# A linear-attention front without casts on GpSimd, and a kept table of ranks for some 250 tasks of a list planner

## The chip, the cores and the metric

The kernel runs on one core of one Trainium2 chip. The metric is device time in microseconds of that core, the median of several executions; lower is better. Times inside the kernel come from one profiled execution, and are counted from its start.

## The reference, cut to what matters

```
phi(x) = where(x > 0, x, exp(x) - 1) + 1                     # q, k, v: (8, 8, 576, 64) fp32
kv  = einsum('bhsd,bhse->bhde', phi(k), v);  z = phi(k).sum(over s)
x   = (phi(q) @ kv) / (phi(q) . z + 1e-6)  -> (4608, 512)     # rows: batch and position, columns: head and dim
P   = exp(x @ w_gate - max), then 8 rounds of column and row normalisation (Sinkhorn), scaled by N/E
out = sum over 8 experts e of P[:, e] * (relu(x @ w1[e]) @ w2[e])   # w1: (8, 512, 1024), w2: (8, 1024, 512)
```

phi(x) is computed as max(x + 1, min(exp(x), 1)).

## The kernel before, in words

The work falls into a front, expert 0, and experts 1 to 7. The front is linear attention. Its unit is the function `att(b, g)`, called 16 times, once for each half of the heads (g) of each batch (b); n = 2b + g numbers the calls, and one call is called a block here. A block loads k, q and v (576 KB each on the page's count), applies phi to k and q, casts v to fp16 into a tile `vv` that has an extra column of ones, and then runs, on TensorE (PE):

- `kv_ps` (line 306, 18 matmuls): the k-v product and the sum of phi(k), copied to `kvz`;
- `qt_ps` (line 332, 9 transposes): phi(q) turned, copied to `qpT` in two parts of 5 and 4;
- `den_ps` (line 347, 10 matmuls), whose reciprocal is `rden`, and `num_ps` (line 371, 10 matmuls);
- `xn` = `num_ps` times `rden` on VectorE (DVE, line 376, three instructions), and `xt_ps` (line 387, two times 5 transposes), copied to the big tile `xT`.

phi takes an exp on ScalarE (ACT, line 266), and then either a +1 on ACT (line 272) and two DVE instructions (a minimum, line 275, and a maximum of two fp16 tiles, line 278), or no ACT instruction and the minimum with a pair of fused add-and-max instructions that read the fp32 input (line 281). The planner chooses. In the kernel before, the cast of v is GpSimd's (POOL, line 225 through the helper `copy`) in all 16 blocks.

After each odd batch, `logits` multiplies x by the gate (line 405). After the last one, `sinkhorn` runs its eight rounds, a chain of small DVE instructions with one tiny matmul in each round; it yields `P_sb`.

Expert 0 is plain: for each of 9 groups g of 512 rows, `layer1` makes eight `hq` tiles (line 536, four matmuls of 128x512 each, over the four chunks c of x's 512 columns; ACT takes the relu, line 540), and `unit_plain` makes four `ye` tiles (line 706, eight matmuls each), copied to `acc` and later scaled by P (line 723). These matmuls are what PE does between the small matmuls of the front. A group can start when `xT` holds all its rows and columns. PSUM holds two `hq` tiles, so the third waits for the relu of the first.

Experts 1 to 7 use a seven-product (Strassen-Winograd) form, 12.3 us of PE work in each of 63 units (lines 627 and 809); they read differences of blocks of x from DRAM (`xst`, line 568, stored to `xd`), and differences of the weights (W, T). Their matmuls stand in a written order (the list `order`).

The order of everything else comes from a planner, `_Plan`. Each task has a table of engines it may run on with a cost in us, dependencies, buffers that it takes, and a rank `prio`. `run` simulates the engines: it takes the engine that can start a task soonest, and on it, of the tasks that can start at that moment, the one of lowest rank. The instructions are recorded in that order, so each engine's order is fixed when the kernel is built; on the chip every engine works its list from the top and waits at its head. For blocks the rank is n - 100; for expert 0 it is g plus a fraction (PE) or g - 400 (relu and copies).

Loads of the first two blocks are issued by SP's queue, then w1 of expert 0 (line 207, after the v cast of block 0: `vcast[0]`), blocks 2 and 3, w2 of expert 0 and the gate's weights by POOL's; later blocks by SP's. Thirty-four matmuls on a tile of zeros (`warm`, line 476) fill PE's early idle time; nothing reads their result.

```
            ti = fadd(("pool", 1.0) if n in (2, 3) else ("sp", 0.45), fn, acq=[gr], prio=pr,
                      deps=[w_last[0] if n in (2, 3, 4) else None, in_prev[0]])
...
        tvv.append(fadd(("pool", 1.3), f_v, deps=[ta, tin["v"]],
                        use=[gvv, gin["v"]], prio=pr))
        vcast[n] = tvv[0]
```

Of the kernel before, what the change touches and what calls it, by code (L numbers as in the profile page):

```python
# [10 lines left out]
FP32 = mybir.dt.float32  # L11
FP16 = mybir.dt.float16
# [5 lines left out]
class _Plan:  # L18
# [14 lines left out]
    def add(self, eng, fn, deps=(), prio=0.0, acq=(), use=(), lat=0.0, after=0.0):  # L33

        if isinstance(eng, tuple):
            eng = {eng[0]: eng[1]}
        k = len(self.t)
        t = {"eng": eng, "fn": fn, "prio": prio, "acq": tuple(acq), "lat": lat, "kids": [], "nd": 0,
             "ready": after, "done": None, "id": k}
        self.t.append(t)  # L40
        for d in set(x for x in deps if x is not None):
            self.t[d]["kids"].append(k)
            t["nd"] += 1
        for g in list(acq) + list(use):
            g["users"].append(k)
        return k
# [76 lines left out]
def kernel(  # L123
# [10 lines left out]
    nc = tc.nc  # L134

    B, H, S, D = q.shape
# [4 lines left out]
    P = 128  # L141
    PW = 64
    NJ = S // PW
    NG = N // 512
    NTT = N // P
    NFT = F // P
    NDT = DM // P
# [3 lines left out]
    S_ = _Plan()  # L151
    add = S_.add

    const = ctx.enter_context(tc.tile_pool(name="const", bufs=1))
# [3 lines left out]
    hqp = ctx.enter_context(tc.tile_pool(name="hqp", bufs=2, space=PSUM))  # L158
# [18 lines left out]
    fp = front.enter_context(tc.tile_pool(name="fp", bufs=2))  # L177
# [1 line left out]
    kvz_t = [fp.tile([P, 2, 2, D + 1], FP16, tag=f"kvz{i}", name=f"kvz{i}", bufs=1) for i in range(2)]  # L179

    p_in = {n: S_.pool(2) for n in "kvq"}
    p_e = S_.pool(2)
    p_t = {n: S_.pool(2) for n in "kq"}
    p_vv, p_kvz, p_qpT, p_xn, p_rden = (S_.pool(2) for _ in range(5))
    p_att, p_hq, p_h = S_.pool(2), S_.pool(2), S_.pool(2)
# [33 lines left out]
    def copy(e, dst, src):  # L219
        if e == "act":  # L220
            nc.scalar.copy(out=dst, in_=src)  # L221
        elif e == "dve":
            nc.vector.tensor_copy(out=dst, in_=src)  # L223
        else:
            nc.gpsimd.tensor_copy(out=dst, in_=src)
# [4 lines left out]
    vcast = {}  # L230

    def fadd(*a, **kw):
        t = add(*a, **kw)
        front_ids.append(t)
        return t

    def att(b, g):
        n = 2 * b + g
        pr = n - 100.0
# [7 lines left out]
        gin, tin, gt, tph = {}, {}, {}, {}  # L247
        for nm, ten in (("k", k), ("q", q), ("v", v)):
            gr = gin[nm] = S_.grp(p_in[nm])

            def fn(_, gr=gr, nm=nm, ten=ten):
# [5 lines left out]
                      deps=[w_last[0] if n in (2, 3, 4) else None, in_prev[0]])  # L257
            in_prev[0] = ti
            tin[nm] = fadd(("dma", 1.55), lambda _: None, deps=[ti], use=[gr], prio=pr, lat=2.6)
        for nm in "kq":  # L260
            ge = S_.grp(p_e)
            gt[nm] = S_.grp(p_t[nm])

            def f_e(_, ge=ge, nm=nm):
                ge["tile"] = fp.tile([P, 2, NJ, D], FP16, tag="e", name="e" + nm)
                nc.scalar.activation(out=ge["tile"], in_=gin[nm]["tile"], func=AF.Exp)

            def f_t(e, g_=gt[nm], nm=nm):
                g_["tile"] = fp.tile([P, NJ, 2, D], FP16, tag="t" + nm, name="t" + nm)
                g_["on"] = e  # L270
                if e == "act":
                    nc.scalar.add(out=g_["tile"].rearrange("p j r d -> p r j d"), in_=gin[nm]["tile"], add=1.0)  # L272

            def f_m(_, ge=ge, g_=gt[nm], nm=nm):
                nc.vector.tensor_scalar(out=ge["tile"], in0=ge["tile"], scalar1=1.0, scalar2=None, op0=ALU.min)
                o = g_["tile"].rearrange("p j r d -> p r j d")
                if g_["on"] == "act":
                    nc.vector.tensor_tensor(out=o, in0=o, in1=ge["tile"], op=ALU.max)
                else:
                    for r in range(2):  # L280
                        nc.vector.scalar_tensor_tensor(out=o[:, r], in0=gin[nm]["tile"][:, r], scalar=1.0,  # L281
                                                       in1=ge["tile"][:, r], op0=ALU.add, op1=ALU.max)
            te = fadd(("act", 1.17), f_e, deps=[tin[nm]], acq=[ge], use=[gin[nm]], prio=pr)
            tt_ = fadd({"dve": 0.6, "act": 1.17}, f_t, deps=[tin[nm]],
                       acq=[gt[nm]], use=[gin[nm]], prio=pr)
            tph[nm] = fadd(("dve", 1.35), f_m, deps=[te, tt_], use=[ge, gt[nm], gin[nm]], prio=pr)
        gvv = S_.grp(p_vv)
        tvv = []
# [3 lines left out]
        ta = fadd(("none", 0.0), f_va, deps=[tin["v"]], acq=[gvv], prio=pr)  # L292
        def f_v(e):
            copy(e, gvv["tile"][:, :, :, 0:D], gin["v"]["tile"])
        tvv.append(fadd(("pool", 1.3), f_v, deps=[ta, tin["v"]],
                        use=[gvv, gin["v"]], prio=pr))
        vcast[n] = tvv[0]
        gkv, gz = [S_.grp(p_ye[2]), S_.grp(p_ye[3])], S_.grp(p_kvz)

        def f_kv(_):  # L300
# [25 lines left out]
        for j0, j1 in ((0, 5), (5, NJ)):  # L326
# [8 lines left out]
            def f_qc(e, j0=j0, j1=j1, gp=gp):  # L335
                copy(e, gq["tile"][:, :, j0:j1, :].rearrange("p h j w -> p j h w"), gp["tile"][:, 0:j1 - j0])
            t1 = fadd(("pe", 0.06 * (j1 - j0)), f_qt, deps=[tph["q"], tqa], acq=[gp], use=[gt["q"]], prio=pr)
            tq.append(fadd({"act": 0.12 + 0.1 * (j1 - j0), "dve": 0.17 + 0.057 * (j1 - j0)}, f_qc, deps=[t1, tqa],
                           use=[gp, gq], prio=pr))
# [23 lines left out]
        for i0, i1 in ((0, 2), (2, 4), (4, 5)):  # L363
# [15 lines left out]
            t1 = fadd(("pe", 0.12 * (i1 - i0)), f_num, deps=[tden, txa], acq=[gn], use=[gq, gz], prio=pr)  # L379
            txn.append(fadd(("dve", 0.14 + 0.275 * (i1 - i0)), f_xn, deps=[t1, trd, txa], use=[gn, grd, gxn], prio=pr))  # L380
        for c2 in range(2):
# [10 lines left out]
            t1 = fadd(("pe", 0.3), f_xt, deps=txn, acq=[gx], use=[gxn], prio=pr)  # L392
# [68 lines left out]
        return add(("dve", 0.8), f_p, deps=last, prio=-200.0)  # L461

    nc.vector.memset(ones_t, 1.0)
    warm = const.tile([P, 512], FP16, tag="warm", name="warm")
    nc.vector.memset(warm, 0.0)

# [18 lines left out]
    for i in range(2):  # L485
        nc.vector.memset(vv_t[i][:, :, :, D], 1.0)
        nc.vector.memset(kvz_t[i], 0.0)
    att(0, 0)
    att(0, 1)
    w_t = {0: load_w1(0, prio=-290.0, parts=2, deps=[vcast[0]])}  # L490
    for b in range(1, B):
        att(b, 0)
        att(b, 1)
        if b == 1:
            w_t[0] += load_w2(0, prio=-96.5, parts=2, deps=[in_prev[0]])
        if b % 2 == 1:
            logits(b // 2)
# [17 lines left out]
    prev_hq = [None]  # L515
# [4 lines left out]
    def layer1(e, g):  # L520
        gw1, tw1, gw2, tw2 = w_t[e]
        bs = range(512 * g // S, (512 * g + 511) // S + 1)
        xd_ = [xt_done[(b, c)] for b in bs for c in range(NDT)]
        th = []
        gh = S_.grp(p_h)

        def f_ha(_):
            gh["tile"] = hpool.tile([P, NFT, 512], FP16, tag="h", name="h")
        tha = add(("none", 0.0), f_ha, deps=[prev_hq[0]], acq=[gh], prio=g - 400.0)
        for f in range(NFT):  # L530
            ghq = S_.grp(p_hq)

            def f_hq(_, f=f, ghq=ghq):
                ghq["tile"] = hqp.tile([P, 512], FP32, tag="hq", name="hq")
                for c in range(NDT):
                    nc.tensor.matmul(ghq["tile"], lhsT=gw1["tile"][:, c, ts(f, P)], rhs=xT[:, c, ds(512 * g, 512)],  # L536
                                     start=(c == 0), stop=(c == NDT - 1))

            def f_rl(_, f=f, ghq=ghq):
                nc.scalar.activation(out=gh["tile"][:, f, :], in_=ghq["tile"], func=AF.Relu)  # L540
            t1 = add(("pe", 0.87), f_hq, deps=[tw1[f // 4], prev_hq[0]] + xd_, acq=[ghq], use=[gw1],
                     prio=g + 0.1 * f + 0.35)
            prev_hq[0] = t1
            x_users.append(t1)
            th.append(add(("act", 0.6), f_rl, deps=[t1, tha], use=[ghq, gh], prio=g - 400.0))
        return gh, [th, th]

# [147 lines left out]
    def unit_plain(e, g, gW=None, tW=None):  # L695
        gw1, tw1, gw2, tw2 = w_t[e]
        gh, th = layer1(e, g) if e == 0 else block7(e, g, gW, tW)
        gy = [S_.grp(p_ye[tt % 2]) for tt in range(4)]
        ty = [None] * 4
# [191 lines left out]
                chain.append(pe_id[key])  # L891
    for d, k_ in zip(chain, chain[1:]):
        S_.dep(k_, d)
    S_.run()


# [28 lines left out]
```

The softmax here doesn't subtract the row's maximum and nothing guards it: scores larger than these inputs give would overflow.

## Time and profile before

| quantity | value |
|---|---|
| time, median of 3 runs | 981.78 us (981.58 to 981.99) |
| span of the profiled execution | 982.2 us |
| PE busy | 962.2 us, 98% |
| PE weight loads busy | 792.7 us, 81% |
| DVE busy | 771.7 us, 79% |
| ACT busy | 563.2 us, 57% |
| POOL busy | 127.9 us, 13% |
| POOL casts of v (line 225), 16 | 19.8 us, 1238 ns each |

The busy shares are of the whole span; the front is its first seventh. A matmul's end is modelled in the profile and successive matmuls overlap in the pipe, so a busy PE may still be running below its pace: the distance from one start to the next tells more than the busy share.

### The profile page before, as it was taken

Reading aid. Unit: us, or ns where it says so; the run is one execution under the profiler, and the core shown is the slowest. Engines: PE = TensorE matmul, PEld = TensorE weight load, DVE = VectorE, ACT = ScalarE, POOL = GpSimd, SP = SyncE. Lnnn points to the kernel's source line nnn. Section 1 sums busy time; section 2 is a strip of 40 time slices with the busy share of each in tenths; the row PEclk is TensorE's granted clock in tenths of the full one; section 3 lists DMA queues with packets and bytes.
Section 4 is the critical chain, followed back from the end, with each engine's and each line's share of the span. In section 5 each row is a group of like instructions: output and inputs, shape, how many; then the busy total and the mean of one; then the engine's idle time right before and its main releaser. Section 6 shows DMA issues by size and latency. Waiting matters only on the chain.

```text
span 982.2 us, 21403 instructions
## 1 busy us (share of the span) xinstructions
PE 962.2 (98%) x8716; PEld 792.7 (81%) x8716; DVE 771.7 (79%) x1561; ACT 563.2 (57%) x1034; POOL 127.9 (13%) x171
## 2 busy tenths in 40 slices
PE   7899999999999999999999999999999999999997
PEld 4455564488888888888888888888888888888885
DVE  6898869967777777777777777777777777777774
ACT  4798754565555555555555555555555555555552
POOL 4111200001111111111111111111111111111110
PEclk9999999999999999999999999999999999999999
DMA  9886953162226312272225322272225322236663
GB/s 318 257 303 239 265 160 140 65 127 77 75 76 142 97 73 76 76 161 76 77 75 137 101 76 75 76 162 76 76 76 137 102 76 76 76 103 168 161 161 98
DMA packets 47029, 121.99 MB, mean 124 GB/s; under 512 B 4177, under 2 KB 18001, under 8 KB 46929
## 3 DMA queue, kind: packets, MB, share of 16 engines
q1 hardware_dynamic: 32128, 99.76, 30.3%
q0 software_dynamic: 14480, 20.33, 11.5%
q8 instruction: 68, 1.11, 0.5%
q10 hardware_dynamic: 320, 0.52, 0.1%
q14 instruction: 33, 0.26, 0.1%
HBM read 119.69 MB, written 17.69 MB: 140 GB/s over the span
## 4 chain that ended last, share of the span: by engine, by line
PE 89%; DVE 1%; ACT 1%; issue 0%
PE ye L809 33%; PE hq L627 23%; PE att L627 11%; PE Zye L627 6%; PE Zye L809 6%; PE ye L706 5%; PE hq L536 4%; PE xt_ps L387 0%; PE kv_ps L306 0%; PE num_ps L371 0%; PE lg_ps L405 0%; DVE tk L281 0%; PE qt_ps L332 0%; ACT tq L272 0%; PE den_ps L347 0%; ACT qpT L221 0%
## 5 line engine op out<-in xcount | busy, mean ns | idle before, releaser
L823 DVE SCALAR_TENSOR_TENSOR acc<-ye,P_sb,acc 128x256 f32<-128x256 f32 x620 | 264.9, 477 | 95.3 <-PE ye L809 77.9
L627 PEld LDWEIGHTS <-W 128*128 128x128 f16 x2016 | 197.1, 98 | 23.7
L809 PEld LDWEIGHTS <-S 128*128 128x128 f16 x1984 | 194.1, 98 | 22.7 <-issue 0.3
L809 PE MATMUL ye<-T,S 128*128 128x256 f16 x1488 | 192.8, 273 | 0.1
L833 POOL TENSOR_TENSOR acc<-acc,st 128x256 f32<-128x256 f32 x124 | 87.5, 725 | 625.6 <-ACT st L830 620.7
L653 ACT ACTIVATE h<-hq 128x512 f16<-128x512 f32 x126 | 76.3, 606 | 160.8 <-PE hq L627 160.8
L627 PEld LDWEIGHTS <-w 128*128 128x128 f16 x1512 | 147.6, 98 | 23.3 <-issue 1.0
L809 PEld LDWEIGHTS <-h 128*128 128x128 f16 x1488 | 145.6, 98 | 16.8
L627 PE MATMUL hq<-xs,W 128*128 128x256 f16 x1008 | 151.2, 273 | 0.0
L627 PE MATMUL att<-xs,W 128*128 128x256 f16 x1008 | 151.2, 272 | 0.0
L627 PE MATMUL hq<-xs,w 128*128 128x256 f16 x1008 | 140.7, 272 | 0.8 <-DVE h L656 0.8
L782 DVE TENSOR_TENSOR S<-h 128x1024 f16<-128x1024 f16 x124 | 85.4, 688 | 57.9 <-ACT h L653 57.9
L656 DVE CUSTOM_DVE_ANT_0 h<-att,s 128x512 f16<-128x512 f32 x126 | 86.7, 688 | 13.1 <-ACT s L643 13.1
L830 ACT ACTIVATE st<-Zye,P_sb 128x256 f32<-128x256 f32 x124 | 52.1, 471 | 78.0 <-PE Zye L809 78.0
L643 ACT COPY s<-hq 128x512 f32<-128x512 f32 x126 | 75.0, 595 | 36.7 <-PE hq L627 36.7
L650 ACT ACTIVATE h<-Zye 128x512 f16<-128x512 f32 x126 | 75.2, 597 | 35.1 <-PE Zye L627 35.1
L656 DVE CUSTOM_DVE_ANT_0 h<-hq,s 128x512 f16<-128x512 f32 x126 | 86.5, 686 | 0.8 <-PE hq L627 0.7
L639 ACT COPY Zye<-hq 128x512 f32<-128x512 f32 x126 | 73.3, 581 | 16.3 <-PE hq L627 16.3
L706 PE MATMUL ye<-w,h 128*128 128x512 f16 x320 | 77.6, 379 | 0.9 <-DVE acc L223 0.9
L627 PE MATMUL Zye<-xs,w 128*128 128x256 f16 x504 | 75.6, 273 | 0.0
L647 ACT COPY s<-att 128x512 f32<-128x512 f32 x126 | 74.5, 591 | 0.0
L536 PE MATMUL hq<-xT,w 128*128 128x512 f16 x288 | 70.6, 379 | 2.4 <-ACT h L540 2.2
(90 smaller groups left out, 963.1 us busy)
## 6 DMA issues: line engine op xcount, KB each, us to landing
xs<-xd SPq DMA_DIRECT2D x63, 896.0 KB, 4.6
w<-in_moe_w_dram POOLq DMA_DIRECT2D x14, 1024.0 KB, 11.7
out_dram<-acc SPq DMA_DIRECT2D x68, 128.0 KB, 2.4
kin<-in_k_dram SPq DMA_DIRECT2D x14, 576.0 KB, 6.0
qin<-in_q_dram SPq DMA_DIRECT2D x14, 576.0 KB, 5.0
vin<-in_v_dram SPq DMA_DIRECT2D x14, 576.0 KB, 6.4
xd<-xst SPq DMA_DIRECT2D x9, 512.0 KB, 2.6
xd<-xT SPq DMA_DIRECT2D x9, 256.0 KB, 7.1
```

Source lines behind the costliest of these rows:

```text
L536: nc.tensor.matmul(ghq["tile"], lhsT=gw1["tile"][:, c, ts(f, P)], rhs=xT[:, c, ds(512 * g, 512)], start=(c == 0), stop=(c == NDT - 1))
L627: nc.tensor.matmul(dst[:, p, :], lhsT=lhs(p, c), rhs=rhs(c), start=(first and p == 0 and c == 0), stop=(c == 1), skip_group_check=True)
L643: nc.scalar.copy(out=gs2["tile"], in_=gX["tile"])
L647: nc.scalar.copy(out=gs5["tile"], in_=gR["tile"])
L650: nc.scalar.activation(out=hd(0, 0), in_=Zt[1], func=AF.Relu)
L653: nc.scalar.activation(out=hd(1, 0), in_=gX["tile"], func=AF.Relu)
L656: nc.vector._custom_dve(TENSOR_ADD_SAT, out=dst, in0=ps, in1=sb, s0=3.0e38, s1=0.0)
L706: nc.tensor.matmul(gy[tt]["tile"], lhsT=gh["tile"][:, f, ds(P * tt, P)], rhs=gw2["tile"][:, f, :], start=(f == 0), stop=(f == NFT - 1))
L782: nc.vector.tensor_tensor(out=Sx[:, i], in0=a0, in1=a1, op=op)
L809: nc.tensor.matmul(bank(g_)[:, s, :], lhsT=lhs(s, kk), rhs=rhs(kk), start=(new and s == 0 and kk == 0), stop=(kk == 3), skip_group_check=True)
L823: nc.vector.scalar_tensor_tensor(out=dst(), in0=bank(g_)[:, s, :], scalar=P_sb[:, gg, e:e + 1], in1=dst(), op0=ALU.mult, op1=ALU.add)
L833: nc.gpsimd.tensor_tensor(out=dst(), in0=dst(), in1=gst["tile"], op=ALU.add)
```

## The change

Seven edits, all in the front, in expert 0's first layer, or in ranks.

1. The cast of v leaves POOL: ACT does it in blocks 0 and 1, DVE in the other 14.
2. The load of w1 waited for block 0's cast on POOL. In its place POOL copies a sliver of that v (128x4) to a tile `gate`, and the load waits for that.
3. The exp tiles `e` have three buffers, not two.
4. In expert 0's group 0, the first two `hq` tiles are each made in two halves: chunks 0 and 1 for both tiles, then chunks 2 and 3 for both.
5. In group 0 a task waits for the first c1 entries of the list of `xT` parts instead of for all of it.
6. A table gives 255 tasks, by number, a new rank, and pins 49 of them to DVE or ACT where the planner had the choice.
7. The two halves of w2's load no longer stand side by side in POOL's queue: the gate's weights are issued between them (this follows from the ranks).

Counted in the built programs, the table and the planner move these instructions besides the casts: `qpT` copies of 5, from 8 on DVE and 8 on ACT to 4 and 12; `kvz` copies, from 30 on DVE and 34 on ACT to 22 and 42; `xT` copies, from 16 and 16 to 18 and 14; the +1 of phi on ACT (with the two-instruction form on DVE), from 13 to 11, so that the pair on line 281 runs 21 times and not 19. PE has the same instructions in another order.

```diff
-    p_e = S_.pool(2)
+    p_e = S_.pool(3)
...
-                ge["tile"] = fp.tile([P, 2, NJ, D], FP16, tag="e", name="e" + nm)
+                ge["tile"] = fp.tile([P, 2, NJ, D], FP16, tag="e", name="e" + nm, bufs=3)
...
-        tvv.append(fadd(("pool", 1.3), f_v, deps=[ta, tin["v"]],
+        tvv.append(fadd(("act", 1.17) if n < 2 else ("dve", 0.75), f_v, deps=[ta, tin["v"]],
                         use=[gvv, gin["v"]], prio=pr))
-        vcast[n] = tvv[0]
+        if n == 0:
+            def f_gate(_):
+                nc.gpsimd.tensor_copy(out=gate, in_=gin["v"]["tile"][:, 0, 0, 0:4])
+            vcast[0] = add(("pool", 0.15), f_gate, deps=[tin["v"]], use=[gin["v"]], prio=pr)
...
-        for f in range(NFT):
-            ghq = S_.grp(p_hq)
...
+        ghqs = [S_.grp(p_hq) for f in range(NFT)]
+        jobs = [(f, 0, NDT) for f in range(NFT)]
+        if g == 0:
+            jobs = [(f, c, c + 2) for c in (0, 2) for f in range(2)] + jobs[2:]
+        for f, c0, c1 in jobs:
+            ghq = ghqs[f]
...
-            t1 = add(("pe", 0.87), f_hq, deps=[tw1[f // 4], prev_hq[0]] + xd_, acq=[ghq], use=[gw1],
+            t1 = add(("pe", 0.2175 * (c1 - c0)), f_hq, deps=[tw1[f // 4], prev_hq[0]] + xd_[0:c1 if g == 0 else None],
+                     acq=[ghq] if c0 == 0 else [], use=[gw1] + ([ghq] if c0 > 0 else []),
                      prio=g + 0.1 * f + 0.35)
...
+    ranks = """
+        45:-99.0012 56:-97.0015:act 65:-96.9982 67:-94.9997 68:-98.9991 73:-94.9994 74:-94.9991:dve
...
+    """
+    for w in ranks.split():
+        n, p, *en = w.split(":")
+        t = S_.t[int(n)]
+        t["prio"] = float(p)
+        if en:
+            t["eng"] = {en[0]: t["eng"][en[0]]}
     S_.run()
```

## The prediction

> **What bounds the kernel now.** I read the table of stretches first, cut where the stages change: before expert 0's first `hq`, to its first `ye`, to the last gap of PE in the front, to the last transposes, to expert 1's first matmul, to its first line 809, and the rest.
>
> ```profile
> core 0: us, PE busy (x) PEld busy (x) DVE busy (x) ACT busy (x) POOL busy (x), PEclk, DMA share, GB/s
> 0.00:22.50 22.50, 17.05 (x148) 9.15 (x149) 15.77 (x34) 9.51 (x14) 11.06 (x19) 0.92 0.99 311
> 22.50:36.40 13.90, 10.57 (x101) 5.47 (x99) 11.36 (x22) 10.49 (x18) 2.73 (x2) 1.00 1.15 317
> 36.40:113.90 77.50, 72.34 (x795) 44.64 (x793) 69.10 (x144) 69.13 (x110) 16.27 (x14) 1.00 0.78 266
> 113.90:137.20 23.30, 23.13 (x278) 15.13 (x279) 14.84 (x38) 12.87 (x25) 0.08 (x1) 1.00 0.77 153
> 137.20:194.30 57.10, 57.10 (x343) 28.19 (x341) 52.58 (x145) 28.05 (x49) 0.00 (x0) 1.00 0.33 127
> ```
>
> After 113.9 us PE has no gap worth naming. So time can only be won where PE runs below its pace before that. Pace, from the timeline: eight `ye` matmuls took 1.89 us and four 1.02, so 0.217 each; one of 18 `kv_ps` 0.034, a transpose or `num_ps` 0.056, a `den_ps` 0.027 (starts divided the same way). Up to the last transposes: 164 `hq` and 136 `ye` (65), 288 `kv_ps` (9.9), 464 transposes and `num_ps` (26), 160 `den_ps` (4.3) and two sets of gate matmuls (1.8), together 107 of 137.3 us. PE lost 30.3 us: 14.9 by 20 us, 5.3 from 20 to 30, and 10.1 from 30 to 113.9 (the stretch less its counts times the pace). The zeros of line 476 count as lost.
>
> Next, the timeline of all engines where the losses are:
>
> ```profile
> 22.53 0.99 PE L536 MATMUL hq<-xT,w 128*128 128x512 f16 x3
> 23.68 1.24 PE L536 MATMUL hq<-xT,w 128*128 128x512 f16 x5 [0.16 <-ACT xT L221]
> 26.29 1.02 PE L536 MATMUL hq<-xT,w 128*128 128x512 f16 x4 [1.36 <-ACT h L540]
> 27.24 0.69 PE L306 MATMUL kv_ps<-vv,tk 64*128 64x130 f16 x18
> 29.49 0.68 PE L332 MATMUL qt_ps<-ident,tq 128*128 128x128 f16 x9 [1.55 <-DVE tq L281]
> ...
> 25.23 1.43 DVE L281 SCALAR_TENSOR_TENSOR tk<-kin,ek 128x576 f16<-128x576 f32 x2
> 27.06 2.37 DVE L281 SCALAR_TENSOR_TENSOR tq<-qin,eq 128x576 f16<-128x576 f32 x2
> 27.25 1.58 POOL L225 CAST vv<-vin 128x1152 f16<-128x1152 f32 x1 [3.15 <-DMA vin<-in_v_dram]
> ...
> 12.39 1.15 POOL L225 CAST vv<-vin 128x1152 f16<-128x1152 f32 x1 [0.28 <-DMA vin<-in_v_dram]
> 12.41 2.40 DVE L281 SCALAR_TENSOR_TENSOR tk<-kin,ek 128x576 f16<-128x576 f32 x2
> ```
>
> The reader is to see two things. The third `hq` waits for a relu that stands behind two exps on ACT. And the pair of line 281 takes 1.43 us, but 2.40 and 2.37 beside a cast on POOL. I went through all 16 casts: eight (at 7.9, 12.4, 27.3, 41.7, 59.3, 64.8, 76.3, 111.1) meet a DVE instruction that is longer than its kind by 0.99, 0.98, 0.94, 0.95, 0.88, 0.55, 0.97 and 0.83: 7.1, or 7.3 us of DVE with small ones. PE's gaps at 43.3, 61.7, 64.1, 78.0 to 79.1 and 113.0, just behind five of them, sum to 4.65 of the 10.1 us.
>
> **What the Trainium skill says.** SBUF — State Buffer, section "SBUF: two separate sides": DVE and GpSimd share a port pair as an exclusive lock; a DVE instruction with two SBUF inputs, or in a two-port mode, and a GpSimd one block each other for the whole instruction. The trace agrees: 0.55 to 0.99 us added, and a `xn`, which reads PSUM, beside the cast at 93.6 keeps its 0.69. VectorE: DVE Perf Modes, section "The perf-mode tier table", has fp32 copies in SBUF at two elements a cycle, which with its 150 fixed cycles makes 1152 elements 0.76 us, an estimate; before has no such copy. TensorE: Matmul & The Clock Gate, "Part 1": half clock after idle stretches; the page shows a PEclk of 0.92 in the first stretch, so one window.
>
> **The change part by part.** Sums are against the span of 982.2; the runs' median is 981.8, so I subtract from that.
>
> *Casts.* Off POOL: DVE gets 7.3 us back. On DVE: 14 times 0.76, +10.6. Bounds for one: 0.48 (line 723's 512 fp32 elements) scaled by 640/2 cycles more gives 0.81; the pair on line 281, one element a cycle, gives 1.36; below it is 0.45 (line 275, fp16). I take 0.76. On ACT: 2 times 1.16. The pinned choices: DVE loses 8 `kvz` (1.75) and 4 `qpT` (1.86), gets 2 `xT` (0.9) and 2 pairs for short forms (1.5). Net DVE +2.1 on 111.1 busy by 137.2; ACT +2.3+1.7+2.8-1.3-2.3 = +3.2 on 102. Both have room only if the idle time at the start is used.
>
> *The start*, walked through with before's durations in the new order. ACT: exp k 4.91, +1 6.38, exp q 7.45, cast 8.52 to 9.68, so `kv_ps` starts at 9.75 (9.12 before): a loss of 0.6, hidden, because `qt_ps` (10.90 before) now has its `tq` at 9.9. DVE: no block from the cast, so block 1's `tk` ends at 12.7 (14.8), its `tq` is made at 15.4 (18.2), block 1's `kv_ps` runs at 14.65 (17.4). Block 0's `xn` waits behind `tq` and ends at 17.0 (16.9). Block 1's `den_ps` 18.05 (19.5), `xn` to 20.5 (22.1). First `hq` halves at 21.15 (22.53): **1.4 gained**. What is queued behind the casts on ACT is exp k of block 1, due at 9.4, and nothing waits for it sooner than 10.8.
>
> *Halves and relus.* The halves need block 0's `xT` alone, so block 1's two copies hide under 0.87 us of matmul. Relus then follow after one exp: third and fourth `hq` at 23.25 and 24.1. DVE: block 2's `tk` 23.5, `tq` 25.4, cast to 26.15 (v landed at 22.8: no wait), `kv_ps` 26.2, `qt_ps` done 27.1. By then 16 `hq` matmuls are done, where before has 12 at 30.0: 30.87 against 27.1, **3.8 gained in all**. Carrying on, block 3's `kv_ps` comes out at 30.4 (33.6).
>
> *Gate, w1, loads.* The sliver lets w1 be issued some 0.9 earlier, but the DMA share is about 1 until 36 us (k, q, v land 1.5 apart) and w1's first half landed at 14.9, six us before use: nothing. Its bytes may push block 1's q and v (10.9, 12.3) by under 1 us; used at 12.35 and 13.4: nothing. w2 split by the gate's weights: first `ye` is PE's at about 31.6, w2's half landed at 29.5: nothing. Third `e` buffer: frees ACT from waits such as the 1.9 us at 9.46, already in the walk. Blocks 4 on are loaded when buffers free, 3 to 4 us sooner.
>
> *From 30 to 113.9.* The 4.65 us behind collisions should go; the twelve casts left add waits of their own where `kv_ps` follows closely. I take **3.5**; both ends: 0 (new waits eat it) and 10.1.
>
> Sum 7.3. A check from the order: before the last transposes PE now does 5.2 us more `hq` and `ye` work (172 and 152 matmuls against 164 and 136, 24 times 0.217). If the front ended at 137.3 as before, 5.2 would be won; 7.3 asks it to end 2.1 earlier, with 2.1 more DVE work, thus 4.2 less idle of 26. The walk finds that before 36 us.
>
> **Rivals.**
> (a) The middle gives it back: DVE and ACT are at 89% from 36 to 114 and get more work, and in-order queues stall on the cast. 3.8 from the start, nothing from the middle, and a quarter of the 5.3 us that the two engines get, 1.3, is paid by PE: 979.3 (978 to 981.5). For it: 0.89 busy; against: the collisions that go.
> (b) PE runs gapless from 30: 3.8+10.1 = 13.9, 967.9. Against: `hq` has two buffers and waits for relus behind 1.16 us exps.
> (c) Slower: DVE binds up to the hand-over to expert 1. From the last transposes (137.2) to 207.8, just ahead of the first line 809, DVE is busy 52.6+7.3, or 59.9 of 70.6, and it does Sinkhorn and P's scaling in order. If the cast is not in the fast mode and costs 1.36, DVE's net is +10.5; less the 3.8 of the start, that comes out at the hand-over, +6.7: 988.5. It decides from a cast of 0.88 us (net 3.8) upwards. Against: line 723 shows fp32 at 0.48 for 512 elements; for: `vv`'s rows are 65 wide.
> (d) The table does nothing, as the losses only move: 981.8.
>
> **How the numbers follow.** Chances: forecast 0.62 (its own range 970 to 978), (a) 0.18, (b) 0.08, (c) 0.07, (d) 0.05. Predicted 974.5. The range leaves out most of (b) and (c): 969.5 to 980.5, which takes in (a). 0.2% is 2 us, about what this measurement can tell: faster is the forecast, (b) and 0.14 of (a), 0.84; same 0.09; slower 0.07.
>
> **What would show it.** DVE's casts near 0.76 us; the line 281 pairs at 1.43 throughout; first `hq` at 21 to 21.5; block 2's `kv_ps` near 26; the last transposes at 134 to 136; no gap above 0.5 us between 140 and 210. It is wrong if the cast takes over 0.9, if PE's gaps from 30 to 114 still sum to 10, if the clock drops in a second window, or if line 809 first waits for DVE's S.

## The result, and the profile after

The changed kernel takes 988.99 us (988.59 to 989.32) against 981.7 for the kernel before in the same comparison: a ratio of 1.0074, 95% interval 1.0056 to 1.0091. It is slower; forecast were 974.5 us and a range that ended at 980.5. Single executions differ by several us: the profiled one of the kernel before took 983.97 us, 2.3 above its median, that of the changed kernel 989.32, 0.3 above its own, so the profiled spans (982.2 and 987.5 us) differ by 5.3 us where the medians differ by 7.3.

The same table of stretches as shown for the kernel before, of the changed kernel:

```profile
core 0: us, PE busy (x) PEld busy (x) DVE busy (x) ACT busy (x) POOL busy (x), PEclk, DMA share, GB/s
0.00:22.50 22.50, 16.46 (x152) 8.95 (x153) 14.32 (x35) 14.22 (x19) 9.66 (x19) 1.00 0.98 307
22.50:36.40 13.90, 9.62 (x91) 5.03 (x90) 10.44 (x21) 9.39 (x18) 1.04 (x2) 0.99 1.16 303
36.40:113.90 77.50, 70.72 (x735) 42.13 (x735) 61.42 (x128) 61.38 (x102) 0.00 (x0) 0.94 0.79 242
113.90:137.20 23.30, 23.12 (x252) 14.23 (x252) 19.05 (x43) 17.62 (x33) 0.00 (x0) 1.00 0.68 228
137.20:194.30 57.10, 57.10 (x413) 30.30 (x410) 47.23 (x131) 28.97 (x53) 0.00 (x0) 1.00 0.36 134
```

From 36.4 to 113.9 us PE ran 735 matmuls where it ran 795 before, DVE's busy time fell from 69.1 to 61.4 although it had taken over fourteen casts, and the granted clock was 0.94. So DVE is not the bound there: everything stood still somewhere. One more cut of the same view finds the place:

```profile
22.50:32.90 10.40, 9.25 (x91) 4.94 (x90) 9.02 (x18) 8.71 (x17) 1.04 (x2) 1.00 1.16 308
32.90:45.00 12.10, 4.42 (x19) 2.21 (x18) 1.84 (x5) 1.36 (x3) 0.00 (x0) 0.64 1.11 281
45.00:113.90 68.90, 66.66 (x720) 40.01 (x718) 61.00 (x127) 60.69 (x101) 0.00 (x0) 0.99 0.75 238
```

In 12 us there are 19 matmuls, 5 instructions on DVE and 3 on ACT, at a clock of 0.64, while the DMA share (the time of all DMA packets as a share of 16 engines' time) is 1.11. PE's timeline of the changed kernel says what it waited for (in brackets the idle time ahead of an instruction, and what ended it):

```profile
21.82 1.89 PE L545 MATMUL hq<-xT,w 128*128 128x512 f16 x8
23.97 1.89 PE L545 MATMUL hq<-xT,w 128*128 128x512 f16 x8 [0.25 <-ACT h L549]
26.93 0.69 PE L309 MATMUL kv_ps<-vv,tk 64*128 64x130 f16 x18 [0.27 <-DVE vv L223]
...
32.24 1.02 PE L545 MATMUL hq<-xT,w 128*128 128x512 f16 x4
40.94 1.87 PE L718 MATMUL ye<-w,h 128*128 128x512 f16 x4 [7.68 <-DMA w<-in_moe_w_dram]
42.60 1.17 PE L335 MATMUL qt_ps<-ident,tq 128*128 128x128 f16 x9
43.56 1.92 PE L718 MATMUL ye<-w,h 128*128 128x512 f16 x4
```

The first lines are what the prediction walked through. Then the first `ye` waits 7.68 us for a half of w2, and the matmuls behind it take nearly twice their time: four cost 1.87 us where four took 1.02. The clock read in stretches of 2 us is 0.50 from 38 to 46. In the kernel before, the first `ye` did not wait:

```profile
35.58 1.02 PE L706 MATMUL ye<-w,h 128*128 128x512 f16 x4
```

The table of waits (us in total, times, longest) shows the other engines stopped behind that one instruction, since PE works in order and the next transposes stand behind `ye`:

```profile
ACT qpT L221 <- PE qt_ps L335: 10.5, 2, 9.5
DVE qpT L223 <- PE qt_ps L335: 9.5, 1, 9.5
PE ye L718 <- DMA w<-in_moe_w_dram: 7.7, 1, 7.7
```

Why the half was late is seen on POOL, whose queue issues these loads. First the kernel before:

```profile
17.49 1.51 POOL L207 DMA_DIRECT2D w<-in_moe_w_dram  x2
19.26 0.75 POOL L471 DMA_DIRECT2D wg_sb<-in_moe_w_gate_dram  x1 [0.26 <-DMA kin<-in_k_dram]
...
112.35 1.63 POOL L207 DMA_DIRECT2D w<-in_moe_w_dram  x2
```

and the changed kernel:

```profile
17.90 0.77 POOL L207 DMA_DIRECT2D w<-in_moe_w_dram  x1
18.64 0.78 POOL L475 DMA_DIRECT2D wg_sb<-in_moe_w_gate_dram  x1
20.03 0.74 POOL L207 DMA_DIRECT2D w<-in_moe_w_dram  x1 [0.60 <-DMA kin<-in_k_dram]
21.91 0.74 POOL L207 DMA_DIRECT2D w<-in_moe_w_dram  x1 [1.14 <-DMA qin<-in_q_dram]
23.42 0.88 POOL L207 DMA_DIRECT2D w<-in_moe_w_dram  x1 [0.77 <-DMA vin<-in_v_dram]
```

Three things differ. The load at 17.90 is w2's *second* half and the one at 20.03 its *first* (the addresses in the built program tell): the table's entry for task 195 gives the first half's issue a rank behind task 197's, the second half's. The gate's weights stand between, because the entry for task 663 moves their rank from -90 to -99.0003. And the loads at 21.91 and 23.42 are expert 1's w1 and w2, which the kernel before issued at 112.35: they had stood in POOL's queue behind casts that waited for v, and the planner's start times of 110 and 115 us for them order the plan but hold nothing back on the chip. The edit list ahead of the prediction has the gate's weights between the halves, but not the exchange and not the early loads. By the completion events the second half landed at 31.87 us, the gate's weights at 35.21 and the first half at 40.90 (before: first half 29.52, second 33.81, gate's weights 37.32). DVE ran five instructions from 32.9 to 45 us, so its new casts did not hold the load back there.

### The profile page after: what moved, and what is told of

Read it like the earlier page. It is cut to its first block, busy times and chain, and to the rows that moved or that the text cites. A ratio compares the mean times of both kernels' runs of the same rounds, so it can differ in the third digit from the quotient of the medians.

```text
span 987.5 us, 21377 instructions
## 1 busy us (share of the span) xinstructions
PE 964.1 (98%) x8716; PEld 792.5 (80%) x8716; DVE 771.7 (78%) x1565; ACT 566.3 (57%) x1046; POOL 111.7 (11%) x156
## 3 DMA queue, kind: packets, MB, share of 16 engines
q8 instruction: 68, 1.11, 0.5%
## 4 chain that ended last, share of the span: by engine, by line
PE 92%; DMA 4%; ACT 2%; DVE 2%; issue 1%; POOL 0%; ACTq 0%; POOLq 0%
PE ye L821 33%; PE hq L639 23%; PE att L639 11%; PE ye L718 6%; PE Zye L639 6%; PE Zye L821 5%; PE hq L545 5%; DMA w<-in_moe_w_dram 2%; DMA kin<-in_k_dram 1%; PE num_ps L374 1%; PE xt_ps L390 1%; PE kv_ps L309 1%; PE qt_ps L335 1%; DVE h L668 0%; ACT qpT L221 0%
## 5 line engine op out<-in xcount | busy, mean ns | idle before, releaser
L821 PEld LDWEIGHTS <-S 128*128 128x128 f16 x1984 | 194.1, 98 | 22.5
L655 ACT COPY s<-hq 128x512 f32<-128x512 f32 x126 | 75.1, 596 | 36.2 <-PE hq L639 36.2
L718 PE MATMUL ye<-w,h 128*128 128x512 f16 x320 | 80.0, 386 | 7.7 <-DMA w<-in_moe_w_dram 7.7
## 6 DMA issues: line engine op xcount, KB each, us to landing
w<-in_moe_w_dram POOLq DMA_DIRECT2D x14, 1024.0 KB, 12.5
```

Source lines behind the costliest of these rows:

```text
L655: nc.scalar.copy(out=gs2["tile"], in_=gX["tile"])
L718: nc.tensor.matmul(gy[tt]["tile"], lhsT=gh["tile"][:, f, ds(P * tt, P)], rhs=gw2["tile"][:, f, :], start=(f == 0), stop=(f == NFT - 1))
L821: nc.tensor.matmul(bank(g_)[:, s, :], lhsT=lhs(s, kk), rhs=rhs(kk), start=(new and s == 0 and kk == 0), stop=(kk == 3), skip_group_check=True)
```

## Experiments

PE's loss is counted below as in the prediction: from one matmul's start to the next, less the pace of its form.

The theories. A: exchange of the halves and the early loads of expert 1 together make the wait. B: the exchange alone does. C, the rival: the load on DVE and ACT takes the time, whatever w2 does. D: the gate's weights in front of a half hold it up. E: SP's loads of blocks 4 and 5, running beside, hold it up. The last two columns are from the profiled execution of each kernel.

| kernel | median us | ratio to before (95%) | half of w2 that lands last, and when | PE waits for it |
|---|---|---|---|---|
| before | 981.7 to 982.08 | | second, 33.81 | none |
| after | 988.99 | 1.0074 (1.0056 to 1.0091) | first, 40.90 | 7.68 |
| hold | 988.38 | 1.0059 (1.0036 to 1.0081) | first, 41.10 | 7.72 |
| halves | 986.05 | 1.0035 (1.0027 to 1.0043) | second, 39.5 | 3.32 |
| both | 985.65 | 1.0027 (1.0013 to 1.0041) | second, 40.9 | 4.68 |
| order | 984.59 | 1.0024 (1.0015 to 1.0033) | second, 37.69 | 1.58 |
| fixed | 981.48 | 0.9990 (0.9983 to 0.9997) | second, 37.67 | 1.76 |
| better | 978.29 | 0.9964 (0.9952 to 0.9977) | second, 32.88 | none |
| before_dve | 990.5 | 1.0075 (1.0054 to 1.0097) | second, 35.84 | none |
| before_dve_hold | 985.72 | 1.0036 (1.0023 to 1.0049) | second, 35.86 | none |
| before_swap | 983.86 | 1.0017 (1.0009 to 1.0025) | first, 36.01 | 1.45 |
| fixed_pool | 980.92 | 0.9997 (0.9985 to 1.0008) | second, 38.40 | 1.91 |
| hold_notable | 982.34 | 1.0004 (0.9996 to 1.0011) | second, 36.74 | 0.4 |
| fixed_joined | 980.62 | 0.9984 (0.9978 to 0.9991) | second, 37.85 | 1.81 |

**hold: expert 1's loads kept back.** POOL copies a sliver of batch 5's `xT` ahead of the load, which keeps its queue until 122.9 us.

```diff
+ nm == "w1" and e == 1 and nc.gpsimd.tensor_copy(out=gate, in_=xT[:, 3, 5 * S:5 * S + 4])
  nc.gpsimd.dma_start(out=dst, ...)
```

> The changed kernel, with one GpSimd copy of 128x4 elements of a late piece of xT (batch 5) ahead of the load of expert 1's w1, so that both loads of expert 1 wait on GpSimd's queue until about 100 us, as they did behind the casts in the kernel before. Theory A (the 7.7 us wait of the first ye comes from two things together: the halves of expert 0's w2 change places, so that the first ye needs the one that is issued last, and expert 1's loads, let go at 22 us, share the DMA engines with it): the half lands at about 34.5 instead of 40.9, the wait shrinks to 1 to 2.5 us, PE's clock stays up, 979 to 982. Theory B (only the exchange of the halves counts, because transfers are served in the order of issue): no change, 988 to 990. Theory C (the start is right but DVE's and ACT's added work takes it back later whatever the loads do): the wait goes but the total stays above 983.

The half landed no sooner, and 0.6 us came back, well within the intervals, as B expected. The early loads do not cause the wait: they stand behind the half in the same queue. The part of A that blamed them for it fell.

**halves: the exchange undone,** the gate's weights still between the halves, expert 1's loads still early; and **both**, with hold as well.

```diff
+ i = 1 - i if nm == "w2" and e == 0 else i
  dst, a, off = g["tile"], [list(x) for x in ap], e * DM * F
```

> The changed kernel with w2's halves of expert 0 issued in their natural order (the addresses of the two issues exchanged; every engine's order is the same), and expert 1's loads still let go early. Theory A: the first ye finds its half at 31.9 and does not wait; the second half comes at 40.9, and the first ye that needs it, some 2 us later, waits 4 to 6 us: 984 to 988. Theory B: nothing waits longer than 1 us, 975 to 980.

> Both of these: expert 1's loads held, and the halves in natural order. Theory A: no wait on w2 above 1 us, no second half-clock window, the 2.5 us that the start won by 30 us stay, and 30 to 114 us lose about what they lost before or 1 to 3 us less: 975 to 979. Theory B: the same as the run with the halves alone. Theory C: 981 to 984.

The first `ye` finds its half, and the wait moves to the second (PE's timeline of halves):

```profile
39.55 1.17 PE L718 MATMUL ye<-w,h 128*128 128x512 f16 x4 [3.32 <-DMA w<-in_moe_w_dram]
```

From after to halves 2.9 us come back and the wait falls from 7.68 to 3.32, so the exchange is a part. (From hold to both it is 2.7, with intervals that overlap a little.) But B had no wait over 1 us left in halves, and A had both at 975 to 979, where it took 985.65. Whichever half goes last lands near 40 us, so neither A nor B is the whole.

**order and fixed: first half, second half, gate's weights.** order has that queue with expert 1's loads early, fixed with them held.

```diff
+ late = nm == "w2" and e == 0; i = {0: 9, 1: 0, 2: 1}[i] if late else i
+ i == 0 and late and pend.append(lambda: fn(_, 2))
+ if i == 9: return wg_now()          # w2's two halves, then the gate's weights
```

> The same order of the three issues, but expert 1's loads let go early as in the changed kernel. Theory D: 2.5 to 3.5 us faster than the run halves (986.05), 982.5 to 984; the loads of expert 1 keep costing 1 to 2 us through blocks 4 and 5, whose inputs land 4 to 8 us later (compare with fixed). Theory E: 986.

> The changed kernel with expert 1's loads held as in the run called hold, and GpSimd's three issues put in the order first half of w2, second half, gate's weights. Every other engine's order is the changed kernel's. New theory D (in the run with both mends the second half still landed at 40.9, because the gate's weights, 8 KB in tiny packets, stand in front of it in GpSimd's queue, and took from 31.8 to 35.3): halves land at about 31.8 and 36 to 37.5, PE's wait for w2 shrinks from 4.8 us to 0.5 to 2, total 980 to 982.5. Theory E (the half is late because SP's loads of blocks 4 and 5, issued 2 us sooner than before, share the DMA engines with it; the gate's load is of no matter): it lands at 39 to 41 all the same, 985 to 986.

In fixed, PE waits only

```profile
37.72 1.02 PE L721 MATMUL ye<-w,h 128*128 128x512 f16 x4 [1.76 <-DMA w<-in_moe_w_dram]
```

From both to fixed 4.2 us come back: D holds. With the early loads (halves to order) it is 1.5 us, less than the 2.5 to 3.5 expected. From hold to fixed only the order of three issues differs, and it is worth 6.9 us (988.38 to 981.48), nearly all of the loss, with the casts and every pinned choice on DVE and ACT as in the changed kernel. So C fell as an explanation of the 7.3 us. From order to fixed, with the wait for w2 nearly the same, holding expert 1's loads is worth 3.1 us. So they do cost, in another place: block 5's inputs landed at 39.4, 43.5 and 47.5 us in order and at 39.05, 40.8 and 42.3 in fixed, and PE lost 3.29 us from 50 to 60 instead of 1.36. In the changed kernel they cost no more than the 0.6 us of hold, which the noise covers: that PE stood waiting for w2 meanwhile fits this, but no run shows it by itself.

**before_dve and before_dve_hold: casts alone.** The kernel before with the casts of blocks 2 to 15 on DVE; then also with expert 1's loads held.

```diff
-            copy(e, gvv["tile"][:, :, :, 0:D], gin["v"]["tile"])
+            copy(e if n < 2 else "dve", gvv["tile"][:, :, :, 0:D], gin["v"]["tile"])
```

> The kernel before with its plan untouched, but the casts of blocks 2 to 15 issued to DVE at the place in the order where they were issued to GpSimd. No table, halves of w2 in order. Theory A: GpSimd's queue is now empty of casts, so expert 1's loads go out at about 21 us; the inputs of blocks 4 and 5 and w2's second half land some 3 to 8 us later than before, and PE waits 1 to 5 us for them: 982 to 986, though DVE gets its 7.3 us of collisions back for 14 casts of 0.75. Theory B: no harm from the loads, 978 to 981.5.

> The run before_dve (the kernel before, casts of blocks 2 to 15 on DVE) with expert 1's two loads held on GpSimd's queue by a copy that waits for a piece of xT of batch 5. If the early loads are the harm in that run: back to 980 to 983, with the inputs of block 5 landing near 41 and not 51. If the cast in DVE's in-order queue is the harm: 987 to 990.

Here 4.8 us hang on the hold by the medians (3.8 by the ratios): taking the casts off POOL sets expert 1's loads free at 21 us, whatever the ranks. before_dve came out above what either theory allowed, and not by a wait for w2: block 5's inputs landed at 45.5 to 51.4 us, in before_dve_hold at 39.6 to 42.5, and PE lost some 4 us more from 50 to 60. With the hold the moved casts still *cost* 3.7 us (985.72 against about 982.05), between the two expectations, though of the eight collisions only those of blocks 0 and 1, whose casts stayed on POOL, are left. In the profiled executions PE lost 9.5 us from 50 to 120 where the kernel before lost 7.8. One place, DVE's timeline and PE's of before_dve_hold:

```profile
49.01 0.76 DVE L223 CAST vv<-vin 128x1152 f16<-128x1152 f32 x1
50.77 1.43 DVE L281 SCALAR_TENSOR_TENSOR tq<-qin,eq 128x576 f16<-128x576 f32 x2
52.89 1.29 DVE L376 TENSOR_TENSOR xn<-num_ps,rden 128x512 f16<-128x512 f32 x2
...
53.63 0.28 PE L371 MATMUL num_ps<-kvz,qpT 128*128 128x128 f16 x2 [0.91 <-DVE xn L376]
```

and the same place in the kernel before:

```profile
50.06 1.43 DVE L281 SCALAR_TENSOR_TENSOR tq<-qin,eq 128x576 f16<-128x576 f32 x2
52.18 1.62 DVE L376 TENSOR_TENSOR xn<-num_ps,rden 128x512 f16<-128x512 f32 x3
...
52.92 0.28 PE L371 MATMUL num_ps<-kvz,qpT 128*128 128x128 f16 x2 [0.40 <-DVE xn L376]
```

DVE is in order and PE's `num_ps` waits for `xn`. The cast at 49.01 moves `tq` and then `xn` back by 0.71 us, and PE's wait grows from 0.40 to 0.91: a cast in that chain is on the path, where a cast on POOL was beside it.

**fixed_pool: the casts of blocks 2 to 15 back on POOL,** everything else as in fixed.

```diff
-            copy(e, gvv["tile"][:, :, :, 0:D], gin["v"]["tile"])
+            copy(e if n < 2 else "pool", gvv["tile"][:, :, :, 0:D], gin["v"]["tile"])
```

> The run fixed with the casts of blocks 2 to 15 on GpSimd at the same places of the plan. If the collisions cost what the prediction took (0.55 to 0.99 us each for about every second cast, 7.1 in before): DVE loses 10.5 us of casts and gets about 6 of collisions, kv_ps comes later where the cast was just ahead of it; 0.5 to 3 us slower than fixed. If DVE's load is what counts: 1 to 3 us faster than fixed.

Neither expectation came true. The intervals of fixed and fixed_pool overlap, although in fixed_pool six of the fourteen casts again meet a DVE instruction that is longer than its kind, by 4.9 us together. In a plan made for it the move costs nothing that this can measure; it also wins nothing.

**before_swap: the order of the changed kernel in the kernel before.**

```diff
+ late = nm == "w2" and e == 0; late and i == 0 and pend.append(lambda: fn(_, 2))
+ i = {0: 1, 1: 9, 2: 0}[i] if late else i
+ if i == 9: return wg_now()          # second half, gate's weights, first half
```

> The kernel before with one thing changed: POOL issues w2's second half, then the gate's weights, then w2's first half, the order that the changed kernel has; casts, ranks and expert 1's held loads stay as before. If the order of these three transfers is the main cause (theory A/B and D), the first half lands behind the gate's weights, at 38.5 to 41 us where it landed at 29.5, the first ye on PE (35.58 us before) waits 3 to 5.5 us for it, a half-clock window follows that wait, and the time is 986 to 989 us (ratio 1.004 to 1.007). If the order only hurts together with the new plan (rival: the changed kernel's PE reaches ye earlier and has nothing else to do, and before has slack here), the wait is under 2 us and the time within 983 us. If the transfers do not matter (theory C), the time stays at 982 us.

```profile
36.05 1.02 PE L709 MATMUL ye<-w,h 128*128 128x512 f16 x4 [1.45 <-DMA w<-in_moe_w_dram]
```

The mechanism is there at about a third of the expected size, 1.7 us by the ratio, and the middle expectation (the order hurts most in the new plan) came nearest. The half landed at 36.01, not at 40.9, and the gate's weights needed 0.15 us behind the second half, not 3.3. One thing that differs is when SP issues block 4's loads, here and in the changed kernel:

```profile
26.54 0.37 SPq L255 DMA_DIRECT2D kin<-in_k_dram  x1
...
24.45 0.37 SPq L253 DMA_DIRECT2D kin<-in_k_dram  x1
```

By the trace's records of DMA packets, SP's first packet came at 30.2 us here, when the second half and the gate's weights were nearly through, and at 28.0 in the changed kernel, where POOL's queue was still moving both. This speaks for E.

**better: block 4's loads in POOL's queue behind w2,** the gate's weights behind them; the rest as in fixed.

```diff
-                (nc.gpsimd if n in (2, 3) else nc.sync).dma_start(
+                (nc.gpsimd if n in (2, 3, 4) else nc.sync).dma_start(
...
+                n == 4 and nm == "v" and wg_now()
```

> The kernel called fixed, with block 4's three loads issued from POOL's queue behind w2's two halves instead of from SP's queue beside them, and the gate's weights behind block 4. Theory E (SP's loads of block 4 share the transfer engines with w2's second half): w2's second half lands at 33 to 35.5 us where it landed at 37.67, the wait of 1.76 us at the second ye and the half-clock window behind it go, block 4's inputs land at 36 to 40 us where ACT first reads them at 39.3 us, and the time is 978 to 980 us (ratio 0.996 to 0.998). Rival: block 4's or 5's inputs then come late, and PE waits for them between 40 and 55 us instead: 981 to 984 us.

w2's halves landed at 30.35 and 32.88, 2.5 us apart, where the second took 5.67 us in fixed (32.00 to 37.67). The gate's weights stand behind both halves in either kernel, so the difference is SP's: E holds for block 4's loads, beside D. In the Trainium skill, DMA: Bandwidth & Descriptors, section "Queues, rings and completion order", says that each DMA engine takes turns between the queues that have work, a packet at a time. The trace agrees: from 28.5 to 32 us in fixed POOL's queue moved 328 packets and SP's 321. A packet of w2 has 1 KB and one of SP's loads 2.25 KB, so POOL's queue got 93 GB/s and SP's 201. The 512 packets of a half went at about 200 per us alone (better, 28 to 30 us) and at about 90 beside SP's; that makes 2.6 and 5.7 us, an estimate that fits the landings. The stretch from 30 to 50 us in the changed kernel:

```profile
30.00:50.00 20.00, 12.11 (x96) 6.82 (x93) 7.50 (x18) 6.91 (x13) 0.00 (x0) 0.74 1.14 274
```

in fixed:

```profile
30.00:50.00 20.00, 18.02 (x186) 10.95 (x184) 14.41 (x31) 14.01 (x25) 0.00 (x0) 0.91 0.84 260
```

and in better:

```profile
30.00:50.00 20.00, 19.76 (x232) 12.07 (x232) 17.49 (x38) 17.00 (x30) 0.00 (x0) 1.00 0.91 304
```

That is 96, 186 and 232 matmuls, at 0.74, 0.91 and 1.00 of the clock; in the kernel before it was

```profile
30.00:50.00 20.00, 18.72 (x209) 11.29 (x207) 16.94 (x34) 15.60 (x28) 2.83 (x2) 1.00 0.81 269
```

The changed kernel with SP's loads put back and nothing else was not run. This version beats both kernels: 978.29 us, 0.36% below the kernel before (0.23 to 0.48%).

**hold_notable: no table of ranks,** expert 1's loads held. Its queue has the halves in order and the gate's weights last.

```diff
-    for w in ranks.split():
-        ...
+ nm == "w1" and e == 1 and nc.gpsimd.tensor_copy(...)      # as in hold
```

> The changed kernel without the table of ranks (the planner's own order for the other edits), with expert 1's loads held to about 113 us as in the kernel before. Its order of issue on POOL is first half, second half, gate's weights. It tells what the structural edits are worth alone. If the casts' move itself costs about 3.5 us (as in before_dve_hold) and the split halves give about 2 us back, 983 to 985 us. If the structural edits carry all that fixed has (ranks worth nothing), 981 to 982 us with no ye wait over 1 us. If the prediction's sum for the parts were right for these edits alone, 977 us or below.

982.34 us, nearest the second expectation: the structural edits without the table, with expert 1's loads held, neither win nor lose. Against hold, which has the table, it is 6.0 us faster; against fixed, which has the table with the three issues put right, the two ratios are 0.14% apart with intervals that touch. So what the table did to the time in this kernel is, within about 1.4 us, what it did to three DMA issues.

**fixed_joined: the first two `hq` in one piece each.**

```diff
-                for c in range(c0, c1):
+                for c in range(0 if c0 == 2 else c0, c1 if c1 == NDT else 0):
```

> The kernel called fixed, with the first two hq of group 0 computed in one piece each at the place of their second halves (the split is undone, order and ranks kept). The prediction's step for the halves said that PE work is pulled ahead to 21.15 us, worth 1.4 us alone. If it holds, the loss of PE by 30 us grows by 1 to 1.7 us and the time is 0.5 to 1.7 us above fixed (982 to 983 us). If the joined work only fills what is otherwise a wait for w2's second half at 35.8 us (rival: the gain at the start is taken back by that wait), the wait for w2 shrinks by the same and the time is that of fixed within 0.5 us.

The first sixteen `hq` matmuls start at 22.01 us in one run instead of in two of eight from 21.82; PE's loss by 30 us is 17.4 us against 17.6 in fixed, and the time is not higher. The wait for w2 did not shrink either (1.81 us against 1.76), so what the second expectation gave as the reason is not seen. The halves are worth nothing that this can measure.

## Why the prediction was wrong

PE's loss in us by stretch, of the profiled executions:

| | 0 to 30 | 30 to 50 | 50 to 120 | sum |
|---|---|---|---|---|
| before | 20.2 | 2.2 | 7.8 | 30.2 |
| after | 17.7 | 10.6 | 6.4 | 34.7 |
| fixed | 17.6 | 4.0 | 5.9 | 27.5 |
| better | 17.4 | 1.1 | 5.2 | 23.7 |

The levels move by up to 1 us with the rounding of the paces, the differences between two rows by about 0.3.

- **"Gate, w1, loads" is the step that failed.** It read that w2 is split by the gate's weights and priced that at nothing, since "w2's half landed at 29.5". That is the landing time of a half that stands first in the queue; the step did not ask which half stood where. The first half landed at 40.90, and the stretch from 30 to 50 lost 8.4 us more than before: the wait of 7.68, and the half clock behind it.
- The same step put no price on "blocks 4 on are loaded when buffers free, 3 to 4 us sooner". Block 4's loads were issued 2.3 to 3.2 us sooner, and better shows that their share of the DMA engines was part of the price: with the DMA share above 1.1 from 22.5 us on, in the very table that the prediction shows, a load moved forward pushed another back.
- It missed that a cast on POOL was also a gate: expert 1's loads stood behind the casts. Worth 4.8 us in before_dve, 3.1 in order, and 0.6 in the changed kernel, which the noise covers.
- **"Casts"** held: the DVE casts took 0.753 us on average (0.76 taken), and the pairs on line 281 took 1.43 us throughout, as here:

```profile
24.78 1.43 DVE L281 SCALAR_TENSOR_TENSOR tq<-qin,eq 128x576 f16<-128x576 f32 x2
26.12 0.76 DVE L223 CAST vv<-vin 128x1152 f16<-128x1152 f32 x1
```

- **"The start" and "Halves and relus"** had the mechanism and were too large: first `hq` at 21.82 (21.15 forecast, 22.53 before), block 2's `kv_ps` at 26.93 (26.2), and 2.5 us gained by 30 us, not 3.8. fixed_joined shows the same gain without the halves.
- **"From 30 to 113.9"** is the term that was mis-sized even without the wait: 3.5 us were taken from collisions going away; from 50 to 120 the changed kernel gained 1.4 us and better 2.6. DVE's collisions are not PE's time one for one (fixed_pool), and casts in DVE's order have a price (before_dve_hold). So the order of the three issues explains the loss, but not all of the miss: with it put right, fixed won 0.5 us and better 3.6 of the 7.3 that were forecast.

The terms close the sum. Forecast was a gain of 7.3, the profiled spans show a loss of 5.3. Of the 12.6 us between them 1.3 lie in the start, 8.4 from 30 to 50, 2.1 from 50 to 120 and 0.2 to 0.7 from 120 to 140, as the paces are rounded: 12.0 to 12.5 in all. The medians lose 2 us more than the spans, for the reason given with the result.

Rival (c) named nearly the time, 988.5, by luck and not by the cause: it needed a cast over 0.88 us and a DVE that binds at the hand-over to expert 1. The cast took 0.753 us, and from 120 us to the last unit of expert 7 PE's matmuls never start more than 0.5 us apart in the changed kernel. The signs listed under "what would show it" worked in part: cast and pairs came out right, the last transposes came at 147.3 us and not at 134 to 136, and "PE's gaps from 30 to 114" showed the error at once.

What stays open: the profiled executions of before and better differ by 5.9 us, their medians by 3.6, since the former lies 2.3 us above its median. In all fourteen traces the `ye` matmuls of experts 1 to 7 take 758.1 to 758.3 us from first to last, so the kernels differ ahead of them; but one execution of each was traced, and where that of the kernel before spent its 2.3 us is not on record.

## What to carry to other kernels

When a table of ranks or a planner reorders work, list every DMA issue of each queue in the new order, with what each loads and who needs it first; here the order of three issues of 0.75 us each cost 6.9 us, where all the other edits together, with expert 1's loads held, won 0.5. An instruction that leaves an in-order queue also releases what stood behind it; ask what that is, and what it will share the DMA engines with. Where the DMA share stands above 1, as here from 22.5 to 45 us, ask which load pays for one that is moved earlier; moving the load that can wait (block 4's k, landed at 31.4 us in fixed and read at 39.3) behind the one that cannot gave the largest gain here.

## What the runs showed of the hardware that was not expected

- A load of 8 KB can hold a queue for 3.3 us. The gate's weights (8 KB, by the trace 512 packets of 16 bytes) landed 3.34 us behind the load ahead of them in the changed kernel and 3.5 in the kernel before; in before_swap 0.15 us. In the first two SP's queue had work beside them: the small packets ran from 27.5 to 34.8 us with SP's from 28.0, and from 30.1 to 36.8 with SP's from 30.2. In before_swap they ran from 28.2 to 30.1, and SP's began at 30.2. That SP's packets are the reason was not tried by itself.
- A wait of 7.68 us cost more than itself: the clock was at half from 36.2 to 46.5 us, 10.2 us, of which 5.6 lay behind the wait. In the Trainium skill, TensorE: Matmul & The Clock Gate, "Part 1", gives windows of 3.4 us. The trace agrees: three of them make 10.2, and the front of the kernel before had one, at 11.7 to 15.1. How many follow a wait is not settled by its length: in hold a wait of 7.72 us had two (37.8 to 44.7); the wait of 1.76 us in fixed had one behind it (38.7 to 42.1), the equal one of 1.81 in fixed_joined none.
